# Startup of a fused retention and MLP kernel: values loaded ahead of the half chunk, decay folded into the queries, plain output copies on two engines, and the weights issued behind the values and the queries

## Chip, cores, metric

One core of one Trainium2 chip. The time of a run is the device time of the launch in microseconds (us), and lower is better. All inputs and the output are fp32; the kernel computes in bf16 with fp32 sums. Every run told of here gave a correct result.

## The reference, cut

```python
# q, k, v: (8 batches, 8 heads, 576 tokens, 64); w_ch1: 512 x 2048; w_ch2: 2048 x 512
gamma = 1 - 2.0 ** (-5 - arange(H))                       # one decay per head
ret   = (q @ k.T / 8) * where(rel >= 0, gamma ** rel, 0)  # rel = position of query - position of key
x     = concat_heads(ret @ v)                             # (8, 576, 512)
u     = x + mix_tokens(x, U, V)                           # token mixing of rank 32
out   = u + relu(u @ w_ch1) @ w_ch2
```

`gamma ** rel` splits into `gamma ** t` for the query and `gamma ** -t` for the key. The kernel multiplies the keys by `gamma ** -t`. The factor `gamma ** t` may go on the queries before the scores, or on the output after them.

Of the kernel before, what the change touches and what calls it, by code (L numbers as in the profile page):

```python
# [34 lines left out]
def kernel(  # L35
# [79 lines left out]
    def early_consts():  # L115
        make_identity(nc, ident)
        nc.gpsimd.memset(lnb, math.log(scale))
        nc.gpsimd.iota(
            posU, pattern=[[2 * P, 4], [1, 2], [0, H]], base=0, channel_multiplier=2,
            allow_small_or_imprecise_dtypes=True,  # L120
        )
        nc.gpsimd.iota(
            iotaU, pattern=[[-1, 2], [1, P]], base=0, channel_multiplier=-2,
            allow_small_or_imprecise_dtypes=True,
        )
        nc.gpsimd.iota(
            pos, pattern=[[P, NI], [0, H]], base=0, channel_multiplier=1,
            allow_small_or_imprecise_dtypes=True,
        )
        make_upper_triangular(nc, tri, val=1.0, diag=True)  # L130
        for h in range(H):
            nc.vector.memset(lngt[:, :, h], lng[h])
        nc.vector.tensor_scalar_add(posU[:, 2:4], posU[:, 2:4], -float(4 * P - HALF))
        nc.vector.tensor_tensor(
            out=posU.rearrange("p u j h -> p (u j) h"),
            in0=lngt[:, 0:8, :], in1=posU.rearrange("p u j h -> p (u j) h"), op=ALU.mult)
        nc.scalar.activation(out=vscaleU, in_=posU, func=AF.Exp, bias=lnb, scale=-1.0)
        nc.vector.tensor_scalar(
            out=triU[0:HALF], in0=iotaU[0:HALF], scalar1=0.0, scalar2=None, op0=ALU.is_ge)
        nc.vector.tensor_scalar(  # L140
            out=triU[HALF:P], in0=iotaU[HALF:P], scalar1=-float(P), scalar2=None,
            op0=ALU.is_ge)
        nc.vector.tensor_scalar_add(pos[:, J + 1:NI, :], pos[:, J + 1:NI, :], -float(S))
        nc.vector.tensor_scalar_add(pos[HALF:P, J, :], pos[HALF:P, J, :], -float(S))
        nc.vector.tensor_tensor(out=lngt, in0=lngt, in1=pos, op=ALU.mult)
        nc.scalar.activation(out=qscale, in_=lngt, func=AF.Exp, bias=0.0, scale=1.0)
        nc.scalar.activation(out=vscale, in_=lngt, func=AF.Exp, bias=lnb, scale=-1.0)
        nc.vector.tensor_copy(out=triH[0:HALF], in_=tri[0:HALF, 0:HALF])
        nc.vector.tensor_copy(out=triH[HALF:P], in_=tri[HALF:P, HALF:P])
        nc.vector.memset(U_E[:, J, :], 0.0)  # L150
        nc.vector.memset(U_O[0:HALF, 0, :], 0.0)
        nc.vector.tensor_copy(out=fan, in_=ident[0:R, None, 0:R].to_broadcast([R, 4, R]))
        nc.vector.tensor_copy(out=swap[:, 0:HALF], in_=ident[:, HALF:P])
        nc.vector.tensor_copy(out=swap[:, HALF:P], in_=ident[:, 0:HALF])
        nc.vector.memset(V4[:, 0:HALF], 0.0)
        nc.vector.memset(V4[:, HALF + S:], 0.0)
        nc.vector.memset(sblk, 0.0)
# [97 lines left out]



    def prep_v(pr, i, rows=slice(0, P)):
        c = ch[pr, i]
        if "v" not in c:  # L260
            c["v"] = v_pool.tile([P, H, D], BF16, tag="v", name="vt")
        scale_rows(c["v"][rows], c["f", 2], i, rows, nc.gpsimd)



# [380 lines left out]
        else:  # L646
            eng.tensor_copy(out=o, in_=f)  # L647

    def scale_u(u, hh, eng):
        o, f = unit_views(u, 1, hh)  # L650
        eng.tensor_tensor(
            out=o, in0=f,
            in1=vscaleU[:, u, :, 4 * hh:4 * hh + 4].rearrange("p j h -> p h j")[
                :, :, :, None].to_broadcast([P, 4, 2, D]),
            op=ALU.mult,
        )
# [101 lines left out]
                start=False, stop=True, skip_group_check=True,  # L758
            )

    def XS_u(u, c0=0, c1=2):
        i0, n = unit_i0(u) + c0, c1 - c0
        nc.vector.tensor_tensor(
            out=st["x", 0][:, i0:i0 + n, :].rearrange("p s (h d) -> p s h d", d=D),
            in0=un[u]["po"][:, c0:c1, :].rearrange("p s (h d) -> p s h d", d=D),
            in1=qscale[:, i0:i0 + n, :, None].to_broadcast([P, n, H, D]), op=ALU.mult,
        )

    def ST_u(u, rows, acc, start):
        for hp in range(NHP):  # L770
            for jj in range(2):
                nc.tensor.matmul(
                    acc[:, hp, :], un[u][1][rows, jj, hp * P:(hp + 1) * P],
# [2 lines left out]
                    skip_group_check=True,  # L776
                )

    def Sblk(acc, slot):
        for hl in range(2):  # L780
            r = slice(hl * HALF, (hl + 1) * HALF)
            nc.scalar.activation(
                out=sblk[r, slot, :, hl * D:(hl + 1) * D],
                in_=acc[r, :, hl * D:(hl + 1) * D], func=AF.Copy)

    def T_J(r):
        c = ch[0, J]
# [77 lines left out]
        return ps_s.tile([P, NHP, P], FP32, tag="pss", name="pss")  # L865

    def cast_unit(u):
        for hh in range(2):
            scale_u(u, hh, nc.gpsimd)
        for hh in range(2):  # L870
            cast_u(u, 0, hh, nc.gpsimd)

    def startup():
        load_u(0, (1, 0))
        load_v_rows()
        load_u(1, (1, 0))
        load(0, J, (1, 0), seg=0)
        load_u(0, (2,))
        load_u(1, (2,))
        load(0, J, (2,), seg=0)  # L880
        load_u_rows()
# [16 lines left out]
        SC_u(0, 0, ps_sc, "psc")  # L898
        mask_u(0, 0)
        cast_unit(1)  # L900
        load_w1(0, 2)
        for u in (0, 1):
            for hh in range(2):
                cast_u(u, 2, hh, nc.gpsimd)
        load_w1(2, 4)
        prep_v(0, J, LO)
        load_w1(4, 6)
        cast_urows()
        load_w1(6, 8)
        cast_qk(0, J, HI, nc.gpsimd, nc.gpsimd)  # L910
        prep_v(0, J, HI)
        T_u(1, 1, nc.scalar)
        SC_u(0, 1, ps_o, "po")
        mask_u(0, 1)
        SC_off(0, ps_sc, "psc")
        warm(3)
        T_u(1, 0, None)
        cast_qk(0, J, LO, nc.scalar, nc.vector, decay=True)
        SC_off(1, ps_o, "po")
        warm(4)  # L920
        SC_u(1, 0, ps_sc, "psc")
        mask_u(1, 0)
        SC_u(1, 1, ps_o, "po")
        mask_u(1, 1)
        T_J(LO)

        acc1 = pss_tile()
        acc2 = ps_big.tile([P, NHP, P], FP32, tag="big", name="pss2")
        ST_u(0, ALL, acc1, True)
        Sblk(acc1, 1)  # L930
        RV_u(0, 0)
        RV_u(0, 1)
        ST_u(0, ALL, acc2, True)
        RV_off()
        XS_u(0)
        SC_J(LO)
        mask_J(LO)
        ST_u(1, LO, acc1, False)
        Sblk(acc1, 2)
        ST_u(1, ALL, acc2, False)  # L940
        Sblk(acc2, 3)
        for u in (2, 3):
            for hh in range(2):
                scale_u(u, hh, nc.gpsimd)
            load_w1(4 * u, 4 * u + 4)
            for hh in range(2):
                cast_u(u, 0, hh, nc.gpsimd)
            if u == 3:
                load_w2(0)
                load_w2(2)  # L950
            cast_u(u, 2, 0, nc.gpsimd)
            cast_u(u, 2, 1, nc.gpsimd)
        for f in range(4, NF, 2):
            load_w2(f)
        RV_u(1, 0)
        RV_u(1, 1)
        QS_u(1, 0, 1)
        QS_u(1, 1, 2)
        XS_u(1)
        RV_J(LO)  # L960
        QS_J(3)
        XS_J(LO)

# [30 lines left out]
    def first_stretch():  # L994
# [13 lines left out]
        make_u()  # L1008
        SC_J(HI)
        mask_J(HI)  # L1010
        y(1)
        acc = pss_tile()
        ST_J(HI, acc)
        Sblk(acc, 0)
# [107 lines left out]
```

## The kernel before: what the change touches

The batches go in pairs. Everything here concerns the first pair. Its tokens are four **units** of 256 (units zero and one of the first batch, two and three of the second), and a **half chunk** of 64 tokens at the end of each batch (`J`; `LO` of the first batch, `HI` of the second). SyncE loads keys, queries and values of a unit as six pieces of 128x512 fp32 (256 KB). GpSimd turns them into bf16 and also issues the loads of the weights. An engine works through its list in order, so **a weight load that stands behind a cast in GpSimd's list is issued only when that cast has had its data**.

`w_ch1` is consumed in 16 slices, f = 0 to 15, of 256 KB each in fp32; `load_w1(a, b)` loads slices a to b-1. I number its calls in the order of their slices: the first piece is (0, 2), the third (4, 6). `y(n)` issues the matmuls of the next n slices for the first batch. They fill TensorE between the attention steps of units two and three. When all 16 are done, the "second expansion" begins (the 128x384 matmuls, for the second batch). The position of its first matmul, 54.57 us before, is my yardstick for all that lies ahead of it.

```python
def startup():
    load_u(0, (1, 0)); load_v_rows(); load_u(1, (1, 0))     # SyncE: 1 keys, 0 queries, 2 values
    load(0, J, (1, 0), seg=0)                               # half chunk, keys and queries
    load_u(0, (2,)); load_u(1, (2,)); load(0, J, (2,), seg=0)
    ...                                                     # then all of units two and three
    cast_unit(0)                     # GpSimd: scale keys, cast queries
    ...
    cast_unit(1)
    load_w1(0, 2)                    # first piece of weights
    for u in (0, 1):
        for hh in range(2):
            cast_u(u, 2, hh, nc.gpsimd)                     # values
    load_w1(2, 4)
    prep_v(0, J, LO)
    load_w1(4, 6)                    # third piece
    cast_urows()
    load_w1(6, 8)
    cast_qk(0, J, HI, nc.gpsimd, nc.gpsimd)
    prep_v(0, J, HI)
    ...
    for u in (2, 3):
        for hh in range(2):
            scale_u(u, hh, nc.gpsimd)                       # keys
        load_w1(4 * u, 4 * u + 4)                           # (8, 12), then (12, 16)
        for hh in range(2):
            cast_u(u, 0, hh, nc.gpsimd)                     # queries
        if u == 3: load_w2(0); load_w2(2)
        cast_u(u, 2, 0, nc.gpsimd); cast_u(u, 2, 1, nc.gpsimd)

def XS_u(u, c0=0, c1=2):             # output of a unit, times gamma ** t, PSUM to bf16
    nc.vector.tensor_tensor(out=x[...], in0=po[...], in1=qscale[...], op=mult)

def first_stretch():
    T_J(HI); y(1); make_u(); SC_J(HI); mask_J(HI)
    y(1)
    ST_J(HI, acc); Sblk(acc, 0)      # state of the half chunk
    def unit(u, ...):
        T_u(u, 1, nc.vector)         # transposes of the keys
        T_u(u, 0, nc.scalar)         # transposes of the queries
        y(2)
        SC_u(u, 0, ...); mask_u(u, 0)
        y(1); ...; SC_u(u, 1, ...); y(1); ...
    unit(2, ...); y(1); unit(3, ...); y(1); ...             # cut
```

## Time and profile before

| | before |
|---|---|
| time, median of 3 runs | 326.94 us (326.61 to 327.01) |
| span of the profiled run | 326.0 us |
| TensorE busy | 315.1 us (97%), full from 72 us on |
| outputs of unit zero begin | 16.66 us |
| first slice of the expansion (f = 0) | 24.12 us |
| wait for unit two's queries | 0.94 + 1.41 us, ending at 30.02 |
| TensorE at half clock | once, 30.0 to 33.4 us |
| second expansion begins | 54.57 us |

Positions are from the start of the profiled span. The profiled run took 327.84 us and is not among the three. Weight loads are issued by GpSimd at 12.05, 18.05, 20.17, 21.37, 26.43 and 36.59 us. The lines that carry the rest stand in the prediction.

### The profile page before, as it was taken

What the parts mean: (1) busy time and instruction counts of PE and PEld (TensorE: products, weight loads), DVE (VectorE), ACT (ScalarE), POOL (GpSimd) and SP (SyncE); (2) the same over time, 40 slices, a digit from 0 to 9 for tenths busy, and PEclk for the clock granted to TensorE, in tenths of its full rate; (3) what the DMA queues carried; (4) which work ended last, traced back from release to release, by engine and by line L of the source; (5) the groups of instructions that cost most, each with busy time, mean ns of one, the idle gap of its engine ahead of it and who ended that gap; (6) DMA issues with size and microseconds to landing.
All of it is one profiled execution on the core that took longest, in us unless ns stands there. A gap on an engine that the chain in (4) does not pass through costs nothing.

```text
span 326.0 us, 9119 instructions
## 1 busy us (share of the span) xinstructions
PE 315.1 (97%) x3886; PEld 171.5 (53%) x3886; DVE 169.7 (52%) x331; ACT 144.0 (44%) x326; POOL 101.8 (31%) x169
## 2 busy tenths in 40 slices
PE   8997999999999999999999999999999999999996
PEld 3573545765444444456744444457644444467544
DVE  7662554636645477546754477556744475510012
ACT  3755556894010385048810484058800572047400
POOL 7786752423112733142321523142221500110000
PEclk9998999999999999999999999999999999999999
DMA  7999999995994999979996599969997440340012
GB/s 217 243 198 255 264 201 203 207 193 90 224 206 113 260 171 185 206 182 173 199 202 161 140 183 205 208 157 176 191 202 166 111 68 1 101 112 0 2 74 87
DMA packets 152376, 53.30 MB, mean 163 GB/s; under 512 B 132016, under 2 KB 149808, under 8 KB 152336
## 3 DMA queue, kind: packets, MB, share of 16 engines
q1 hardware_dynamic: 144512, 40.40, 65.1%
q0 software_dynamic: 7824, 12.32, 16.2%
q8 instruction: 30, 0.49, 0.7%
q14 instruction: 10, 0.08, 0.1%
HBM read 36.85 MB, written 9.44 MB: 142 GB/s over the span
## 4 chain that ended last, share of the span: by engine, by line
PE 71%; DMA 15%; SPq 5%; ACT 3%; POOL 2%; DVE 2%; issue 1%; DVEq 0%; POOLq 0%
PE ps_y L565 36%; PE ps_y L531 27%; DMA stage_t<-in_v_dram 8%; DMA stage_t<-in_k_dram 4%; SPq L629 3%; SPq L227 2%; PE pp L312 2%; DVE u L480 2%; DMA stage_t<-in_q_dram 2%; DMA qkT<-qk 1%; ACT y L536 1%; PE pp L332 1%; POOL vt L288 1%; PE ps_y L576 1%; PE pp L344 1%
## 5 line engine op out<-in xcount | busy, mean ns | idle before, releaser
L531 PE MATMUL ps_y<-uT,w_sb 128*128 128x256 bf16 (+2 forms) x768 | 134.3, 328 | 1.6 <-ACT y L536 1.1
L536 ACT ACTIVATE y<-ps_y 128x384 bf16<-128x384 f32 (+2 forms) x192 | 89.6, 491 | 96.1 <-PE ps_y L531 95.0
L565 PE MATMUL ps_y<-w_sb,y 128*128 128x512 bf16 x560 | 126.5, 380 | 0.0
L531 PEld LDWEIGHTS <-w_sb 128*128 128x128 bf16 x768 | 72.7, 98 | 50.3 <-issue 5.0
L565 PEld LDWEIGHTS <-y 128*128 128x128 bf16 x560 | 52.6, 98 | 61.1
L288 POOL TENSOR_TENSOR vt<-stage_t,vscale 64x256 bf16<-64x256 f32 (+1 forms) x81 | 50.3, 621 | 68.7 <-DMA stage_t<-in_v_dram 49.8
L554 DVE TENSOR_TENSOR o_sb<-ps_y,u 128x512 f32<-128x512 f32 (+2 forms) x38 | 25.2, 664 | 82.4 <-PE ps_y L565 80.1
L557 POOL DMA_DIRECT2D out_dram<-o_sb x31 | 17.2, 555 | 108.4 <-DVE o_sb L554 102.6
L320 DVE TENSOR_TENSOR ret<-pp,triH 128x512 bf16<-128x512 f32 x27 | 18.7, 692 | 28.2 <-PE pp L344 20.4
L480 DVE TENSOR_TENSOR u<-ph,xt 128x768 bf16<-128x768 f32 (+2 forms) x24 | 21.8, 951 | 5.9 <-PE ph L474 5.9
L453 ACT ACTIVATE a_sb<-pa 128x128 bf16<-128x128 f32 x8 | 2.2, 278 | 43.8 <-PE pa L447 43.8
L360 DVE TENSOR_TENSOR xt<-pp,qscale 128x512 bf16<-128x512 f32 x27 | 18.6, 689 | 4.7 <-PE pp L344 4.2
L279 DVE CAST qk<-stage_t 64x256 bf16<-64x256 f32 x54 | 19.7, 366 | 1.2
L399 DVE TENSOR_TENSOR s_sb<-AB,Af 64x256 bf16<-64x256 f32 x42 | 17.7, 422 | 2.1 <-ACT s_sb L394 1.5
L354 DVE COPY q<-qkT 64x256 bf16<-64x256 bf16 x48 | 14.0, 293 | 7.5 <-DMA qkT<-qk 6.5
L280 ACT ACTIVATE qk<-stage_t 128x512 bf16<-128x512 f32 x27 | 16.8, 622 | 0.1
L701 DVE TENSOR_TENSOR ret<-psc,triU 128x1024 bf16<-128x1024 f32 x8 | 9.6, 1219 | 10.6 <-PE psc L693 10.6
L392 ACT ACTIVATE Af<-AB 128x256 f32<-128x256 f32 x24 | 9.2, 385 | 7.9 <-PE AB L374 7.4
L647 POOL CAST qk<-stage_t 128x512 bf16<-128x512 f32 x16 | 9.8, 623 | 5.5 <-DMA stage_t<-in_v_dram 2.9
L277 ACT ACTIVATE qk<-stage_t 128x256 bf16<-128x256 f32 x27 | 11.1, 410 | 0.0
L312 PEld LDWEIGHTS <-qkT 64*64 64x64 bf16 x432 | 5.6, 107 | 9.9 <-issue 8.7
L191 PE MATMUL pw<-ident 128*128 128x512 bf16 x27 | 8.8, 473 | 1.4 <-POOL ident masks.py:199 1.4
(120 smaller groups left out, 212.1 us busy)
## 6 DMA issues: line engine op xcount, KB each, us to landing
stage_t<-in_k_dram SPq DMA_DIRECT2D x32, 256.0 KB, 5.0
stage_t<-in_q_dram SPq DMA_DIRECT2D x32, 256.0 KB, 5.5
stage_t<-in_v_dram SPq DMA_DIRECT2D x32, 256.0 KB, 6.0
out_dram<-o_sb POOLq DMA_DIRECT2D x31, 256.0 KB, 3.4
w_sb<-in_moe_w_ch_dram POOLq DMA_DIRECT2D x12, 256.0 KB, 8.1
stage_t<-in_k_dram SPq DMA_DIRECT2D x8, 128.0 KB, 3.8
stage_t<-in_q_dram SPq DMA_DIRECT2D x8, 128.0 KB, 3.4
stage_t<-in_v_dram SPq DMA_DIRECT2D x8, 128.0 KB, 3.6
```

The lines of the kernel that those rows point to most:

```text
L279: nc.vector.tensor_copy(out=o[to, hl], in_=f[fr, hl])
L280: nc.scalar.activation(out=c["qk"][:, 0, :], in_=c["f", 0].rearrange("p h d -> p (h d)"), func=AF.Copy)
L288: nc.gpsimd.tensor_tensor(out=o[to, hl], in0=f[fr, hl], in1=w[fr, hl, :, None].to_broadcast([n, NHP, D]), op=ALU.mult)
L320: nc.vector.tensor_tensor(out=ret.rearrange("p a b i -> p a (b i)").rearrange("p a (b i) -> p a b i", i=D), in0=pp[:, :, 0:NHP * D].rearra ...
L360: nc.vector.tensor_tensor(out=st["x", pr][:, i, :].rearrange("p (hp hl d) -> p hl hp d", hl=2, d=D), in0=pp[:, :, NHP * D:2 * NHP * D].rea ...
L399: nc.vector.tensor_tensor(out=S_[half(x), 1, :], in0=Bk[half(1 - x)], in1=Af[half(1 - x), now, :], op=ALU.add)
L480: nc.vector.tensor_tensor(out=st["u", par][:, i0 - base:i0 - base + n, w].rearrange("p s (c d) -> p c s d", c=2), in0=ph[k][:, :, 0:n, :], ...
L531: nc.tensor.matmul(ps[:, 0:n, :], w1_sb[:, cc, f * P:(f + 1) * P], st["uT", par][:, c0:c0 + n, cc, :], start=(cc == 0), stop=(cc == NCC - 1),)
L536: nc.scalar.activation(out=st["y1", par][:, f, c0 * P:(c0 + n) * P], in_=ps[:, 0:n, :].rearrange("p s t -> p (s t)"), func=AF.Relu)
L554: nc.vector.tensor_tensor(out=o_sb[:, 0:n], in0=ps[:, 0:n], in1=st["u", par][:, c, w], op=ALU.add)
L557: (nc.sync if last else nc.gpsimd).dma_start(out=out_flat[r0:r0 + P, w], in_=o_sb[:, 0:n])
L565: nc.tensor.matmul(ps, st["y1", par][:, f, c * P:(c + 1) * P], w2_sb[:, f, :], start=(f == 0), stop=(f == NF - 1),)
```

## The change

The intent is to shorten the startup and remove the wait for unit two's queries. Values come earlier, the multiply on the way out of PSUM becomes two copies on two engines, unit one (the second unit) is accumulated by halves of the heads, and the first weights leave the loads of the values and queries alone. The core of the diff:

```diff
+        nc.scalar.activation(out=posU, in_=posU, func=AF.Exp, bias=0.0, scale=1.0)   # gamma ** t
     def cast_unit(u):
-        for hh in range(2):
-            scale_u(u, hh, nc.gpsimd)
-        for hh in range(2):
-            cast_u(u, 0, hh, nc.gpsimd)
+        for j in (1, 0):
+            for hh in range(2):
+                scale_u(u, j, hh, nc.gpsimd)
     def XS_u(u):
+        if u < 2:
+            nc.scalar.activation(out=st["x", 0][:, i0, :], in_=un[u]["po"][:, 0, :], func=AF.Copy)
+            nc.vector.tensor_copy(out=st["x", 0][:, i0 + 1, :], in_=un[u]["po"][:, 1, :])
+            return
     def startup():
         load_u(1, (1, 0))
+        load_u(0, (2,))
         load(0, J, (1, 0), seg=0)
-        load_u(0, (2,))
         load_u(1, (2,))
         ...
         cast_unit(1)
-        load_w1(0, 2)
-        for u in (0, 1):  ...cast values...
-        load_w1(2, 4)
-        prep_v(0, J, LO)
-        load_w1(4, 6)
-        cast_urows()
-        load_w1(6, 8)
-        cast_qk(0, J, HI, nc.gpsimd, nc.gpsimd)
-        prep_v(0, J, HI)
+        ...cast values of unit zero, later of unit one; half chunk's values on VectorE...
+        for hh in range(2):
+            ...state and outputs of unit one, by head halves...
+        load_w1(0, 2)
+        cast_urows()
+        load_w1(2, 4)
+        cast_qk(0, J, HI, nc.gpsimd, nc.gpsimd)
+        prep_v(0, J, HI)
         for u in (2, 3):
             ...scale keys...
-            load_w1(4 * u, 4 * u + 4)
+            if u == 3:
+                load_w1(8, 12)
             ...cast queries...
-            if u == 3:
-                load_w2(0)
-                load_w2(2)
+            if u == 2:
+                load_w1(4, 6)
+                load_w1(6, 8)
+            else:
+                load_w1(12, 16)
     def first_stretch():
         mask_J(HI)
-        y(1)
+        y(2)
         acc = pss_tile()
```

Not only the first weights move: the third and fourth pieces go behind the casts of unit two's queries. The kernel also does one slice more, three in place of two, ahead of unit two's transposes.

## The prediction

> **What bounds the kernel now.** I read the page first, parts 2 and 4, then the table of engine times by stretch, then the first 75 us of the timeline and of the chain of waits. Part 2:
>
> ```profile
> PE   8997999999999999999999999999999999999996
> PEclk9998999999999999999999999999999999999999
> DMA  7999999995994999979996599969997440340012
> ```
>
> A slice is 8.15 us. TensorE is full from about 72 us to the end, so nothing that the change does there can count; its work is the same to the matmul (one warm-up matmul fewer). The only dips of TensorE and of its clock lie in the first five slices, where all of the change lies. The stretches of 6 us:
>
> ```profile
> 18.00:24.00 6.00, 5.73 (x135) 4.59 (x132) 3.60 (x5) 2.91 (x8) 5.58 (x10) 1.00 1.11 208
> 24.00:30.00 6.00, 3.55 (x31) 1.68 (x30) 2.25 (x5) 3.33 (x9) 4.38 (x6) 1.00 1.24 262
> 30.00:36.00 6.00, 5.98 (x58) 2.94 (x58) 1.23 (x1) 3.25 (x5) 2.70 (x4) 0.72 1.19 269
> ```
>
> The columns are TensorE, weight loads, VectorE, ScalarE, GpSimd, granted clock, DMA share and GB/s. From 24 to 30 us TensorE does only 3.55 us of work, and from 30 to 36 us it has a granted clock of 0.72. Over 0 to 72 us its busy times sum to 65.6 us, so 6.4 us is all the idle time that there is. Why it idles:
>
> ```profile
> 28.32 0.29 PE L662 MATMUL pst<-ident,qk 128*128 128x128 bf16 x2 [0.94 <-POOL qk L647]
> 29.34 0.62 POOL L647 CAST qk<-stage_t 128x512 bf16<-128x512 f32 x1 [1.07 <-DMA stage_t<-in_q_dram]
> 30.02 0.82 PE L662 MATMUL pst<-ident,qk 128*128 128x128 bf16 x6 [1.41 <-POOL qk L647]
> 30.63 3.26 PE L531 MATMUL ps_y<-uT,w_sb 128*128 128x512 bf16 x8
> ```
>
> TensorE waits for GpSimd's cast of the queries of unit two (the third of four), which waits for their load, landed at 29.3 us. After it, eight 128x512 matmuls take 3.26 us, where four take 1.04 us elsewhere; the low clock costs about 1.2 us here and 1.7 us in all (0.28 of 6 us). So this hole costs some 2.35 + 1.7 = 4 us, the largest prize. Earlier, in the startup:
>
> ```profile
> 15.35 2.34 DVE L701 TENSOR_TENSOR ret<-psc,triU 128x1024 bf16<-128x1024 f32 x2
> 16.66 0.64 PE L720 MATMUL po<-qk,ret 64*128 64x64 bf16 x32
> 19.18 1.03 POOL L252 TENSOR_TENSOR vt<-stage_t,vscale 64x512 bf16<-64x512 f32 x1 [0.38 <-DMA stage_t<-in_v_dram]
> 20.82 1.22 DVE L763 TENSOR_TENSOR xt<-po,qscale 128x1024 bf16<-128x1024 f32 x1 [0.59 <-PE po L755]
> 24.12 1.10 PE L531 MATMUL ps_y<-uT,w_sb 128*128 128x512 bf16 x4 [0.33 <-ACT uT L990]
> ```
>
> From 16.1 to 23.1 us TensorE goes through its startup list with no gap over 0.1 us. It is bound there by its own work once the first mask of unit one has ended (16.56 us; the output tile of unit zero takes that PSUM place, and its first matmul starts at 16.66). The expansion starts at 24.12 us. There is a second bound, in the chain that ended last:
>
> ```profile
> 37.13 12.82 DMA stage_t<-in_v_dram
> 58.29 5.21 DMA stage_t<-in_v_dram
> 65.77 3.56 DMA stage_t<-in_k_dram
> 71.90 2.77 PE ps_y L531 x20
> ```
>
> Before 71.9 us the chain is loads, not TensorE, though TensorE loses only 0.65 us there. A TensorE that comes earlier would wait for these loads of the second batch pair.
>
> **What the Trainium skill says.** (1) "GPSIMD Engine Reference", section 3.1, gives two-input elementwise work on GpSimd about 2.6 cycles per element, because both inputs share a read port, and the best one-input loop 1.8. The trace agrees in direction: the scaling of 128x512 takes 1.058 us and the cast 0.616 us. (2) "PSUM — Partial Sum Buffer", section on bank collisions, says that ScalarE and VectorE must not read the same bank and quadrant at once, but different banks are free. The two halves of the output tile are 128x512 fp32, a bank each. Still the built program makes the VectorE copy wait for the ScalarE copy, so they do not run side by side; the trace has the same pattern where L674 waits 1.34 us for L673. (3) "TensorE: Matmul & The Clock Gate", Part 1, says that the clock halves after an idle window of about 3.4 us and stays so for a window. The trace has one stretch at 0.5, 3.4 us long, after the hole at 28 to 30 us, which had some transposes in it, so it agrees about the length of the slow stretch. (4) "DMA: Bandwidth & Descriptors", section "Queues, rings and completion order", says that each DMA engine takes turns between its queues by packet. The trace agrees: while weights are queued on GpSimd's queue, 512 KB of fp32 lands every 2.8 to 2.9 us (23.56, 26.49, 29.30 us), about 180 GB/s[...].
>
> **The change, part by part.**
>
> Decay in the queries. Four casts of 0.616 us become scalings of 1.058 us on GpSimd. Unit zero's queries end at 8.37 instead of 7.83 us (+0.54); unit one's at 12.56 instead of 12.11 us. Each step after follows: first transposes and scores +0.55, mask zero 10.9, the transposes of unit one's queries 13.2 (12.60 before, a warm-up lies between), their two serial copies end 15.36 (14.76), scores 15.4 (14.81), first mask of unit one 15.95 to 17.15. So the outputs of unit zero start at 17.25 instead of 16.66 us: **+0.6 us on the path**.
>
> Outputs as plain copies. One VectorE multiply of 1.23 us becomes a ScalarE copy of 0.59 and a VectorE copy of 0.69 us, serial: 1.28 us. No gain, and the half chunk's output copy on ScalarE waits behind it: about +0.35 us at the tail.
>
> Values of the half chunk on VectorE. The GpSimd scaling (1.03 us, done 20.22) becomes one of 0.77 us (the like of L240), behind mask, copies and half-chunk masks, done about 21.3 us. Its matmuls, at 20.72 before, come at 21.35. This is mostly the same shift, plus 0.2 us. Sum: the expansion starts at about 25.2 instead of 24.12 us, **+1.1 us**.
>
> Loads. Until 12 us the loads are the same, but the first weights (512 KB of fp32) move from 12.05 to about 17.2 us, and the third and fourth pieces (1 MB) to behind the queries of unit two, about 26.4 us. Values of unit zero land at 12.4 and 13.4 instead of 14.2 and 15.1, which TensorE hardly needs earlier. What counts is the end of unit two's queries. Between 11.44 and 29.29 us before, 4.9 MB went through (276 GB/s); without 1 MB of weights the same takes 14.2 us, so these queries land at about 25.7 and are cast by 26.4. TensorE asks for them at 29.2. **The hole of 2.35 us and its slow clock go: about -4 us.**
>
> What takes its place. A fifth slice of weights (f = 4) is in the third piece, issued 26.4. All six pieces before took 5.5 to 8.7 us to land, so 31.9. TensorE, having done f = 0 to 3, asks for it at 30.6: **a new wait of 1.3 us**. The piece for f = 8 to 11 is issued at about 31.5, behind the fourth (lands 34.8), and needs 5.8 us at 180 GB/s: 40.6; TensorE asks at 39.5: **another 1.1 us**.
>
> Sum: +1.1 - 4 + 1.3 + 1.1 = about **-0.5 us** at 42 us of the trace. I check this with positions: the scores of unit three came at 42.3 us with eight slices done; now they come at 42.4 with nine, each 0.86 us, so -0.75 us. The rest is full TensorE, but for the loads at 69 us, which could take half of it or give another half. I take -0.9 us, leaning a little on the clock staying whole.
>
> **Rivals.**
> 1. The weights are in time. The pieces for f = 4 and f = 8 land before they are asked for. For: SyncE's loads are then further ahead, and GpSimd's queue gets over half of the bandwidth when it has a backlog. Against: every piece took 5.5 us or more. Then -3 us, unless the loads at 69 us hold it: 323.5 to 325.
> 2. The weights are later. The fourth to sixth pieces are queued 5 us later than before, each behind a GpSimd cast that waits for a load. For: the slice of f = 8 was landed 6 us ahead of its use before, so all of that slack is used. Each wait of over 2 us can bring the half clock back for 3.4 us, 1.7 us more. Then +2 to +4 us: 329 to 331.
> 3. Loads bound all up to 72 us. The bytes are the same, and only the dip of DMA share at 17 to 20 us (0.7 to 0.8 against 1.25) can be won, about 1.1 us; the last weights end about 3 us later, since GpSimd's queue begins later. For: the chain of waits names loads. Against: TensorE lost only 0.65 us to them. Then 326 to 328 whatever the startup does.
>
> **Range and chances.** The middle is 326.0 us. Rival 1 sets the low side, 2 and 3 the high side; both are some 2.5 us off, so 323.4 to 328.8. To be faster by over 2%, 6.5 us, nearly all of the idle and slow-clock time (6.4 + 1.7) would have to go: 2%. Slower by 6.5 us needs two long waits for weights with the clock halved: 2%. Within 2%: 96%.
>
> **What would show it.** Right: GpSimd's third and fourth scalings end at about 8.4 us; outputs of unit zero start at 17.2; the expansion starts at 25 us; unit two's queries land before 27 us and TensorE does not wait for their cast; there are waits of 1 to 2 us before the slices f = 4 and f = 8; the VectorE output copy begins where ScalarE's ends. Wrong: an expansion that starts at 24.1 or sooner (then the serial chain was not what set the startup, and the gain is 1 us larger); no wait before f = 4 and f = 8 (rival 1); waits over 2 us there with clock under 1.0 after them (rival 2); a wait of several us at 70 us with no hole before it (rival 3).

## The result

| | before | after |
|---|---|---|
| time, median of 4 runs, the profiled one among them | 326.98 us (326.61 to 327.84) | 332.08 us (331.12 to 333.15) |
| span of the profiled run | 326.0 us | 329.5 us |
| outputs of unit zero begin | 16.66 us | 17.64 us |
| first slice | 24.12 us | 25.99 us |
| wait for unit two's queries | 2.35 us | none |
| wait before slice f = 4 | none | 3.16 us |
| second expansion begins | 54.57 us | 58.25 us |

The ratio is 1.0153 (95% interval 1.0108 to 1.0198). A ratio is the mean time of one kernel's fast runs over that of the other's of the same rounds, so not quite the ratio of the medians. The kernel became about 1.5% slower: inside the 2% class, but 3.3 us above the top of the range.

The page of the kernel after, TensorE, its clock and the DMA share in slices of 8.2 us:

```profile
PE   7797798999999999999999999999999999999996
PEclk9999799999999999999999999999999999999999
DMA  7999999975992999998998599868996542340012
```

TensorE's dip has not gone. It was in the fourth slice and is now in the fourth and fifth, with the reduced clock in the fifth; the second slice, which is the startup, has fallen from 9 to 7. From the eighth slice on the row is as before. By stretches of 6 us (after the window's bounds and its length: TensorE, weight loads, VectorE, ScalarE, GpSimd, then granted clock, DMA share, GB/s):

```profile
12.00:18.00 6.00, 4.89 (x119) 3.29 (x113) 4.13 (x5) 4.93 (x8) 4.06 (x6) 1.00 1.09 164
24.00:30.00 6.00, 5.46 (x68) 2.75 (x68) 2.06 (x4) 3.86 (x9) 3.88 (x5) 1.00 1.22 280
30.00:36.00 6.00, 2.84 (x23) 1.48 (x22) 0.69 (x1) 2.64 (x5) 6.00 (x9) 0.92 1.27 245
```

24 to 30 us is now well filled (5.46, was 3.55), as intended. 30 to 36 us is empty in its place (2.84, was 5.98). The timeline of the kernel after at that point:

```profile
28.84 0.61 POOL L648 CAST qk<-stage_t 128x512 bf16<-128x512 f32 x1 [0.53 <-DMA stage_t<-in_q_dram]
29.40 0.81 POOL L197 DMA_DIRECT2D w_sb<-in_moe_w_ch_dram  x1
...
30.77 1.03 PE L532 MATMUL ps_y<-uT,w_sb 128*128 128x512 bf16 x4
34.95 1.86 PE L532 MATMUL ps_y<-uT,w_sb 128*128 128x512 bf16 x4 [3.16 <-DMA w_sb<-in_moe_w_ch_dram]
```

Read it from the top. The last queries of unit two land and are cast at 28.84. Only then can GpSimd issue the third piece of weights, at 29.40. TensorE is through f = 3 at about 31.8 and waits until 34.95 for slice f = 4 of that piece. That slice then takes 1.86 us instead of 1.03, at half clock. The chain of work that ended last names the same four steps (start, duration, what):

```profile
19.90 8.89 DMA stage_t<-in_q_dram
28.84 0.56 POOL qk L648
29.40 5.51 DMA w_sb<-in_moe_w_ch_dram
34.95 1.86 PE ps_y L532 x4
```

The startup after:

```profile
17.64 0.64 PE L721 MATMUL po<-qk,ret 64*128 64x64 bf16 x32 [0.18 <-DVE ret L702]
...
18.89 0.60 ACT L766 ACTIVATE xt<-po 128x512 bf16<-128x512 f32 x1 [0.36 <-PE po L747]
19.52 0.69 DVE L768 CAST xt<-po 128x512 bf16<-128x512 f32 x1 [0.81 <-ACT xt L766]
...
25.99 1.10 PE L532 MATMUL ps_y<-uT,w_sb 128*128 128x512 bf16 x4 [0.34 <-ACT uT L1001]
```

VectorE's copy begins where ScalarE's ends (18.89 + 0.60) and says so (`<-ACT xt`): the two halves do not run side by side. There is also a wait that I had not foreseen, ahead of the second expansion, in the kernel after and, second, in the one before:

```profile
58.25 1.46 PE L532 MATMUL ps_y<-uT,w_sb 128*128 128x384 bf16 x8 [1.15 <-ACT uT L506]
```
```profile
54.57 1.46 PE L531 MATMUL ps_y<-uT,w_sb 128*128 128x384 bf16 x8 [0.18 <-ACT uT L505]
```

The profiled loss closes by these terms: first slice +1.87, the query wait -2.35, a wait of 0.20 before f = 2, the wait before f = 4 +3.16, the wait at 58 us 1.15 - 0.18 = +0.97. The sum is +3.85. The yardstick moved by 58.25 - 54.57 = 3.68, and the span by 3.5. Each profiled run has one stretch of half clock ahead of 58 us, so that cancels there. The first term is the difference of two single traces. Three edits of each kernel that change nothing ahead of 19 us give its scatter: first slice at 24.12, 24.63, 24.44 and 24.06 us before (with b_fill, b_w68late, b_w4late), and at 25.99, 25.86, 25.68 and 25.62 after (with a_y1, a_warm, a_w34early). The means differ by 1.5 us, and the starts of unit zero's outputs, 16.84 and 17.41 on average, by 0.57.

Over all runs the clock does not cancel. The mean clock of a run shows how many stretches of 3.4 us at half clock it had: none near 1.0, one near 0.995, two (or one of twice the length) near 0.99. Over 43 further runs of the kernel before, on five chips, the mean time was 327.15 us at 1.0 (12 runs), 328.06 at 0.995 (20) and 329.94 at 0.99 (11). The four runs after had 0.993, 0.989, 0.995 and 0.990: one or two stretches, never none. **The times of the same kernel before thus spread over 325.6 to 330.7 us**, and its medians by chip over 327.8 to 329.2. Ratios below are against runs on the same chip.

### The profile page after: what moved, and what is told of

Same layout as the page of the kernel before. It is cut to its first block, busy times and chain, and to the rows that moved or that the text cites. A ratio compares the mean times of both kernels' runs of the same rounds, so it can differ in the third digit from the quotient of the medians.

```text
span 329.5 us, 9122 instructions
## 1 busy us (share of the span) xinstructions
PE 314.5 (95%) x3885; PEld 170.7 (52%) x3885; DVE 169.0 (51%) x333; ACT 144.4 (44%) x327; POOL 103.4 (31%) x169
## 4 chain that ended last, share of the span: by engine, by line
PE 80%; DMA 8%; ACT 4%; SPq 3%; DVE 2%; issue 1%; POOL 1%; DVEq 0%
PE ps_y L566 36%; PE ps_y L532 35%; DMA stage_t<-in_q_dram 3%; SPq L630 2%; DMA stage_t<-in_v_dram 2%; PE pp L313 2%; DMA w_sb<-in_moe_w_ch_dram 2%; DVE u L481 2%; ACT y L537 1%; DMA qkT<-qk 1%; PE pp L333 1%; PE ps_y L577 1%; PE pp L345 1%; PE AB L375 1%; PE pa L448 1%
## 5 line engine op out<-in xcount | busy, mean ns | idle before, releaser
L280 DVE CAST qk<-stage_t 64x256 bf16<-64x256 f32 x54 | 19.5, 360 | 2.0 <-DMA stage_t<-in_k_dram 0.8
L192 PE MATMUL pw<-ident 128*128 128x512 bf16 x26 | 7.9, 446 | 1.4 <-POOL ident masks.py:199 1.4
L652 POOL TENSOR_TENSOR qk<-stage_t,vscaleU 128x512 bf16<-128x512 f32 x8 | 8.4, 1062 | 2.3 <-DMA stage_t<-in_k_dram 1.4
```

The costliest lines, as they stand in the source:

```text
L280: nc.vector.tensor_copy(out=o[to, hl], in_=f[fr, hl])
```

## The experiments

Sixteen kernels ran. Names with `a_` are edits of the kernel after, `b_` of the kernel before, and `c_` are combinations. The theories:

- **Weights:** the loss is the schedule of the weights, above all pieces three and four behind the queries' casts.
- **Startup:** the later first slice (+1.87 us) is what costs.
- **Slice:** the slice spent early is missing at 57 us.
- **Clock:** the half-clock stretch after the wait, not the wait, is the cost.

### The third and fourth pieces early: a_w34early

```diff
         load_w1(2, 4)
+        load_w1(4, 6)
+        load_w1(6, 8)
         ...
-            if u == 2:
-                load_w1(4, 6)
-                load_w1(6, 8)
-            else:
+            if u == 3:
                 load_w1(12, 16)
```

> The changed kernel with the third and fourth weight pieces (slices 4 to 7) issued right behind the second, ahead of the half chunk's casts, not behind unit two's queries. Theory W (the wait for the third piece took the place of the wait for the queries): the piece lands at about 31 instead of 34.9 us, no wait before slice 4; unit two's queries land 1 to 1.5 us later than 28.8, so some 1 us of the old wait comes back; total 327.5 to 329.5. Rival B (only the bytes ahead of TensorE count, whatever their order): what the slice gains the queries lose, total stays 331 to 333. Rival S (the loss is all startup): unchanged, 331 to 333, with no change before 26 us.

Measured: 333.48 us, ratio 1.0167 (1.0114 to 1.022). The wait before f = 4 was gone (that slice at 31.45 us), and a longer one stood before f = 8:

```profile
44.63 3.59 PE L532 MATMUL ps_y<-uT,w_sb 128*128 128x512 bf16 x8 [5.43 <-DMA w_sb<-in_moe_w_ch_dram]
```

The fifth piece was still behind unit three's key scalings, so it was issued at 36.55 and landed at 44.58. Curing one piece moved the wait to the next. The times expected under the theory of the weights, 327.5 to 329.5, did not come: this edit alone cures nothing. The run had 6.8 us at half clock.

### The first piece back in its place: a_w1first

```diff
         cast_unit(1)
+        load_w1(0, 2)
         cast_u(0, 2, 0, nc.gpsimd)
         ...
-        load_w1(0, 2)
         cast_urows()
```

> The changed kernel with the first weight piece back at its old place, ahead of the value casts (about 13 us instead of 18.2). Theory D (between 13 and 20 us SyncE's small loads cannot fill the DMA engines, so the first piece is free there): it lands at about 19, unit two's queries land 1 to 1.9 us earlier (27 to 27.8), the third piece is issued that much earlier, the wait before slice 4 falls from 3.2 to about 1.7 us; total 329.5 to 330.5. Rival B (bytes alone): the values and the half chunk land about 1 us later, the expansion starts about 1 us later, queries as they are; total 331 to 333.

Measured: 328.43 us, ratio 1.0007 (0.9974 to 1.004); one of the four runs, 332.66 us, counted as slow and is not in the ratio. Unit two's queries landed at 25.0 us, not at 28.79, though 512 KB more were queued ahead of them. The third piece was issued at 27.08, and its slice came at 33.46:

```profile
33.46 1.04 PE L532 MATMUL ps_y<-uT,w_sb 128*128 128x512 bf16 x4 [2.73 <-DMA w_sb<-in_moe_w_ch_dram]
```

A wait of 2.73 us, with no half clock in this run. So a large part of the loss depends on where the first piece lies, though less surely than the ratio says. The run left out is the only one of the study; with it the four average 329.26 us, 0.4% over the kernel before. It lies 4.5 us above the other three, and its clock of 0.995 stands for 1.7 of these at most.

What moved through the DMA engines, by queue (packets, MB, share of the time of 16 engines; shares can add up to over 100%). q1 is SyncE's queue, q0 GpSimd's. A piece of weights counts there as 0.26 MB, the bf16 that is written. From 12 to 18 us, the kernel after and then a_w1first:

```profile
q1 hardware_dynamic: 3118, 0.96, 107.4%
```
```profile
q1 hardware_dynamic: 3124, 0.97, 96.9%
q0 software_dynamic: 519, 0.26, 39.0%
```

From 18 to 24 us, in the same order:

```profile
q1 hardware_dynamic: 2488, 0.92, 66.3%
q0 software_dynamic: 508, 0.25, 34.9%
```
```profile
q1 hardware_dynamic: 3202, 1.30, 97.6%
q0 software_dynamic: 125, 0.06, 8.0%
```

From 12 to 18 us SyncE's loads moved as much without the first piece (0.96 MB) as beside it (0.97). **With the piece away, the other loads did not take over its bandwidth.** From 18 to 24 us they moved 0.92 MB beside weights, and 1.30 nearly without. In the kernel after the first two pieces, issued at 18.24 and 19.54 us, were in flight until 25.17 and 28.52, and the last queries of unit two took 8.89 us from issue to landing. In a_w1first the first piece had landed at 19.36, the second was issued only at 20.83, and these queries took 4.96 us. So the change, by issuing the first piece later, put it **beside the queries**. This compares two traces. In a_w1all, below, where the first piece is early too but three more are in flight beside the queries, they landed at 30.41 us.

### The extra slice back: a_y1

```diff
         mask_J(HI)
-        y(2)
+        y(1)
```

> The changed kernel with one slice, as before, ahead of the half chunk's state, not two. Theory W: slice 4 is then asked for one score group later, so the wait falls by some 0.4 us, and one slice more is left to fill the wait at 56 us (1.2 us, was 0.2 us before the change), so about 1 us there: total 1.2 to 2 us below the changed kernel of the same rounds. Rival: the extra slice fills the hole and its absence costs: same or slower.

Measured: 331.68 us, ratio 1.010 (1.0062 to 1.0138). The wait at the second expansion fell to that of the kernel before:

```profile
60.52 1.46 PE L532 MATMUL ps_y<-uT,w_sb 128*128 128x384 bf16 x8 [0.18 <-ACT uT L506]
```

So the extra slice is the cause of that wait of 1.15 us. But the slice was then missing earlier: TensorE waited 0.81 us for the queries and 4.89 us for f = 4. The slice decides where TensorE waits, and hardly how long.

### The startup's decay undone: a_nodecay

```diff
     def XS_u(u):
-        if u < 2:  ...two plain copies...
     def cast_unit(u):
+        ...scale keys, cast queries, as before...
```

> The changed kernel without the decay in the queries: they are cast as before and the outputs of units zero and one take one VectorE multiply. Theory W: the expansion starts 0.6 to 1 us earlier than 26.0, but slice 4 still waits for the third piece that lands at 34.9, so the wait grows by as much and the total stays within 0.5 us. Rival S (startup chain is the loss): total 0.6 to 1.5 us lower.

Measured: 331.97 us, ratio 1.0118 (1.0076 to 1.0159). TensorE was ready for the first slice at 24.67 us, over 1 us earlier than in the kernel after. It waited 0.97 us for the first piece of weights, and 4.75 us for the third. A faster startup ran into the weights, whose third piece landed at 35.99 us. This speaks against the startup theory.

### The first piece late in the kernel before: b_w1late

```diff
-        load_w1(0, 2)
         for u in (0, 1):
             ...cast values...
-        load_w1(2, 4)
+        load_w1(0, 2)
         prep_v(0, J, LO)
-        load_w1(4, 6)
+        load_w1(2, 4)
         cast_urows()
+        load_w1(4, 6)
         load_w1(6, 8)
```

> The kernel before, with only the first weight piece moved behind the four value casts (issued at about 17 us, not 12), the second and third each one place later, all else as it was. Theory D: the startup does not change (the expansion starts at 24 us, or waits a little for the piece), but the 512 KB now lie in the busy time from 20 to 29 us, so unit two's queries land at 30 to 31 us, not 29.3, and the wait grows: total 1 to 4 us over before. Rival B (bytes alone) or 'the weights were in the way of the values': same total or lower.

Measured: 328.73 us, ratio 0.9996 (0.9956 to 1.0036). Unit two's queries landed at 26.68 us, so the expectation of 30 to 31 failed. In this kernel the late first piece did not delay the queries. TensorE waited 0.60 + 0.26 us for them, and then 1.11 + 0.86 + 0.26 us in unit three. From 8 to 24 us it moved as much as the kernel before, 3.52 MB and 3.55. By queue it was SyncE's loads that made up for the piece, with 3.23 MB in place of 2.88 (weights 0.26 in place of 0.64). In this order of loads, then, they did take over its place, though four pieces were issued between 17.8 and 22.4 us. A late first piece alone does not cost time, then, and the loss seen against a_w1first belongs to the kernel after as a whole.

### Decay in the queries alone: b_decay

```diff
     def cast_unit(u):
-        ...scale keys, cast queries...
+        for j in (1, 0):
+            for hh in range(2):
+                scale_u(u, j, hh, nc.gpsimd)
     def XS_u(u, ...):
+        if u < 2:  ...ScalarE copies one half, VectorE the other...
```

> The kernel before with only the decay in the queries and the outputs of units zero and one as two copies. Startup chain: the expansion starts 0.6 to 1.2 us later than 24.1. Theory W/D: the wait for unit two's queries (landed at about 29.3 whatever GpSimd does before) shrinks by as much, total within 0.7 us of before. Rival S: total 0.6 to 1.5 us over before.

Measured: 328.22 us, ratio 0.9963 (0.9914 to 1.0012). The outputs of unit zero began at 17.4 us and the first slice at 25.25, 1.1 us later than before, which is the size predicted. In the time no loss is seen: the interval ends at 1.0012, and the startup theory asked for 0.6 to 1.5 us, 1.0018 at least. So that theory is refuted here. That TensorE loses this time ahead of a wait that it would have had anyway is the explanation I expected, but the profiled run, the slowest of its four, does not show it: the wait there did not shrink but grew, to 0.99 + 2.04 us, since the queries were cast only at 31.23.

### The fourth and sixth pieces later in the kernel before: b_w68late

```diff
         cast_urows()
-        load_w1(6, 8)
         ...
-            load_w1(4 * u, 4 * u + 4)
+            if u == 2:
+                load_w1(6, 8)
+            else:
+                load_w1(12, 16)
             ...cast queries...
+            if u == 2:
+                load_w1(8, 12)
```

> The kernel before with the fourth weight piece (slices 6 and 7) issued behind unit two's key scaling, where the fifth was, and the fifth behind the query casts. Its 512 KB then no longer stand before unit two's queries: by the bytes (270 GB/s) these land 1.9 us sooner, at about 27.4, the wait of 2.35 us falls to about 0.7 and with it perhaps the slow clock (1.7 us). Slices 6 and 7 are asked for at about 36 us and land at 33 to 35, slice 8 at about 39 against 40. Total 1.5 to 3.5 us under before; if slice 8 waits, the same or 1 us over.

Measured: 326.71 us (324.84 to 329.42), ratio 0.9943 (0.9872 to 1.0014). The queries landed at 28.14 us instead of 29.29, which is 1.15 us for 512 KB moved behind them. TensorE waited 0.24 + 0.64 us, and the second expansion began at 51.79, 2.8 us earlier. The best single time of the study is here, but the four runs had 0, 1, 0 and 2 half-clock stretches, and the interval holds 1.

### All weights at the places of the kernel before: a_w1all

```diff
         cast_unit(1)
+        load_w1(0, 2)
         ...
-        load_w1(0, 2)
-        cast_urows()
         load_w1(2, 4)
+        load_w1(4, 6)
+        cast_urows()
+        load_w1(6, 8)
         ...
+            load_w1(4 * u, 4 * u + 4)       # and load_w2 as before
```

> The changed kernel with all weight pieces where the kernel before has them. Theory W/D: no wait for weights; the expansion starts at about 25.5; unit two's queries land at about 29 and TensorE asks for them at about 29.5, so a wait of 1 us or less; 1 us more is lost at 56 us for the slice that was used up. Total within 1.5 us of before (the changed kernel is 5 us over it). Rival S: stays 1.5 to 3 us over before.

Measured: 327.9 us, ratio 0.9982 (0.9936 to 1.0027). All the rest of the change was kept: values ahead, decay, copies on two engines, head halves, the extra slice. The first slice began at 25.64 us, as late as in the kernel after, and the wait was again the one for the queries:

```profile
31.13 0.51 PE L663 MATMUL pst<-ident,qk 128*128 128x128 bf16 x6 [1.25 <-POOL qk L648]
```

The second expansion began at 54.19 us (54.57 before). **This decides between the theories:** the loss is in the schedule of the weights, and all other parts together are worth nothing either way, to within about 0.6%.

### Is it the clock? a_warm

```diff
-            y(2)
+            y(1)
+            if u == 2:
+                ...12 matmuls of 128x512 on the identity, result unused...
+            y(1)
```

> The changed kernel with twelve warm-up matmuls of 128x512 (2.6 us at full clock) between slices 3 and 4, where TensorE waited 3.2 us for the third weight piece. Their result is never read. If the slow clock after the wait is part of the loss, it goes: slices 4 to 6 run at full clock and the total is 1.7 to 3.4 us below the changed kernel (ratio to before 1.005 to 1.010, not 1.015). If the wait alone is the loss, the ratio stays at about 1.015. If the piece comes earlier than in that trace, the warm-ups themselves cost up to 2.6 us.

Measured: 331.93 us, ratio 1.014 (1.0091 to 1.0189). The matmuls lie between f = 3 and f = 4, where TensorE waits. Three of the four runs had a clock of 0.999 to 1.0, and took 332.60, 331.25 and 330.88 us. The fourth, the slowest, had one stretch, and is the one that was profiled. After the twelve matmuls TensorE still waited there for the third piece:

```profile
37.01 1.04 PE L532 MATMUL ps_y<-uT,w_sb 128*128 128x512 bf16 x4 [2.37 <-DMA w_sb<-in_moe_w_ch_dram]
```

These three runs average 331.6 us, 4.4 us above the 327.15 of the kernel before at full clock. So the wait itself costs, and the clock theory explains at most the difference between runs of one kernel.

### Filling the wait of the kernel before with the slice: b_fill

```diff
         mask_J(HI)
-        y(1)
+        y(2)
         ...
-            y(2)
+            y(1 if u == 2 else 2)
```

> The kernel before with the second slice of unit three's... of the third unit's pair (slice 2) moved ahead of the half chunk's state, that is into the wait for the queries; no slice is used up. The wait of 2.35 us falls by one slice, to about 1.4; total 0.9 us under before, and 2.6 under it if the clock then stays whole.

Measured: 326.81 us, ratio 0.9972 (0.9928 to 1.0016). The wait for the queries fell to 1.51 us, with 0.53 us before the scores. It had no half-clock stretch in three of four runs. A gain of 0.3% is suggested, not shown.

### Two combinations that did not settle: c_fill68 and b_vfirst

c_fill68 is b_fill and b_w68late together. b_vfirst is the kernel before with one part of the change alone:

```diff
         load_u(1, (1, 0))
-        load(0, J, (1, 0), seg=0)
         load_u(0, (2,))
+        load(0, J, (1, 0), seg=0)
```

> The same, and the fourth weight piece behind unit two's key scaling and the fifth behind its query casts: the version meant to beat both. The queries land near 28 us, the wait is under 0.5 us, no slow clock, no wait at 56 us; slices 6 and 8 in time. Total 2.5 to 4 us under before (ratio 0.988 to 0.992). If slice 8 then waits for the fifth piece: ratio 0.995 or more.

> The kernel before with only the load order changed: the values of unit zero ahead of the half chunk's keys and queries. TensorE's startup is set by the first mask of unit one and by its own work after it, so nothing is to be had: total within 0.5 us of before. Were the values what held the startup, 0.5 to 1 us less.

Measured: c_fill68 326.23 us (325.31 to 329.73), ratio 0.9977 (0.9931 to 1.0023); its profiled run, the slowest of six, waited 2.98 us for values of unit three. b_vfirst 327.17 us, ratio 0.9982 (0.994 to 1.0024). Neither is told apart from the kernel before.

### The change with its weights one place earlier: a_w34fix

Here the first two pieces stay late, as in the change, but the third to sixth are each issued one place earlier:

```diff
         load_w1(2, 4)
+        load_w1(4, 6)
         cast_qk(0, J, HI, nc.gpsimd, nc.gpsimd)
         ...
             ...scale keys...
-            if u == 3:
-                load_w1(8, 12)
-            ...cast queries...
             if u == 2:
-                load_w1(4, 6)
                 load_w1(6, 8)
             else:
                 load_w1(12, 16)
+            ...cast queries...
+            if u == 2:
+                load_w1(8, 12)
```

> The changed kernel, first two weight pieces late as in the change, but the third right behind the second, the fourth behind unit two's key scaling, the fifth behind its query casts, the sixth behind unit three's key scaling: one place earlier each than in the change. If the loss is that pieces three to six stand behind casts that wait for loads, the third lands at about 31 us and the fifth at about 38 to 40, no wait over 1 us before slices 4 and 8, ratio to before 0.996 to 1.004. If the late first piece is the loss by itself, ratio 1.010 or more.

Measured: 327.4 us (326.64 to 328.89), ratio 0.9961 (0.9907 to 1.0015), all four runs at clock 1.0. The third piece was issued by 19.5 us and landed at 29.3, the fourth at 34.13, the fifth at 38.37. TensorE's waits:

```profile
34.17 1.04 PE L532 MATMUL ps_y<-uT,w_sb 128*128 128x512 bf16 x4 [0.34 <-DMA w_sb<-in_moe_w_ch_dram]
...
38.80 0.28 PE L663 MATMUL pst<-ident,qk 128*128 128x128 bf16 x2 [0.49 <-POOL qk L648]
39.92 0.51 PE L663 MATMUL pst<-ident,qk 128*128 128x128 bf16 x6 [0.84 <-POOL qk L648]
```

0.34 us for a weight, 1.33 us for unit three's queries, none for unit two's. **With a_w1all this is the proof from the side of the kernel after: the order of four weight loads gives back the whole loss.** It also corrects a reading that a_w1first invites: the first piece need not be early. The kernel before drew slow runs on this chip (see b_w4late), but against the mean of all its 43 runs, 328.29 us, these four (mean 327.59) are not slower either, and c_a34 below repeats the result on another chip.

### The change's late weights in the kernel before: b_w4late

```diff
-        load_w1(4, 6)
         cast_urows()
-        load_w1(6, 8)
         ...
-            load_w1(4 * u, 4 * u + 4)
+            if u == 3:
+                load_w1(8, 12)
             ...cast queries...
+            if u == 2:
+                load_w1(4, 6)
+                load_w1(6, 8)
+            else:
+                load_w1(12, 16)              # load_w2 also as in the change
```

> The kernel before, first two weight pieces as they were, but pieces three to six and the last matrix where the change has them, each behind casts that wait for loads. Unit two's queries land 1.5 to 3 us earlier (26.5 to 28); the third piece is issued at about 28 and lands at 33.5 to 35, slice 4 is asked for at about 30.5: a wait of 3 to 4 us in place of the 2.35 us. Ratio to before 1.003 to 1.010. If it is 1.000 or less, the places of pieces three to six cost nothing without the rest of the change.

Measured: 329.53 us, ratio 1.0006 (0.9943 to 1.007). The queries landed at 27.0 us, 2.3 us earlier for 1 MB moved behind them. TensorE waited only 0.27 us for them, and then:

```profile
35.16 1.89 PE L531 MATMUL ps_y<-uT,w_sb 128*128 128x512 bf16 x4 [4.65 <-DMA w_sb<-in_moe_w_ch_dram]
```

The mechanism is the same in a kernel that has nothing else of the change: one wait taken away, a longer one in its place, and half clock after it. The second expansion began at 57.05 us. The **time** does not confirm a loss. On this chip three of the seven runs of the kernel before had two half-clock stretches (median 328.98), so the comparison is against a slow draw and the interval is wide. From the side of the kernel before, the theory rests on the trace alone.

### Towards a better version: c_a34 and c_b68v

c_a34 is a_w34fix with one slice of unit two's filler kept back (`y(1 if u == 2 else 2)`). c_b68v is b_w68late with b_vfirst's order of loads.

> a_w34fix (changed kernel, pieces three to six one place earlier) with one slice fewer in unit three's first filler, so that a slice is left for the wait at 56 us, which was 1.15 us in every kernel that used it up and 0.2 us in the others. If that accounting is right, TensorE's wait there falls to 0.2 us and the total is up to 1 us under a_w34fix (ratio to before 0.992 to 0.996); if the slice only moves the wait to the scores of the third unit, ratio as a_w34fix, 0.996.

> b_w68late (kernel before, fourth and fifth weight pieces one place later) with the values of unit zero ahead of the half chunk's keys and queries. If the fewer bytes ahead of unit two's queries are a real gain (b_w68late gave 0.994, unclear), ratio 0.992 to 0.996 with an interval under 1; if it was a lucky draw of the slow-clock windows, 0.997 to 1.001.

Measured: c_a34 327.26 us (6 runs), ratio 0.997 (0.9928 to 1.0012). Its wait at the second expansion was gone, but it waited 1.35 us for unit three's queries and 0.54 us before scores: again the slice only chose the place. c_b68v 326.59 us (325.51 to 327.99, 6 runs), ratio 0.9952 (0.9905 to 0.9999), with a single wait for unit two's queries left:

```profile
29.49 0.51 PE L662 MATMUL pst<-ident,qk 128*128 128x128 bf16 x6 [0.77 <-POOL qk L647]
```

Its second expansion began at 52.41 us. It is some 0.5% faster than the kernel before, with an interval that just excludes 1 (one of sixteen intervals, so a hint), and some 2% faster than the kernel after if the two ratios are divided (0.9952 / 1.0153 = 0.980, over different chips).

## Why the prediction was wrong

**The reading of what bounds the kernel was right.** All of the difference arose ahead of 58 us (3.68 of it, of 3.5 in the span), and nothing came back or was added behind it.

**The query wait went, as predicted.** It was 2.35 us and became none.

**The step that failed is "these queries land at about 25.7".** They landed at 28.79, only half a microsecond earlier than the 29.29 of before (at 28.44, 29.05 and 29.32 in a_nodecay, a_warm and a_y1, which have the same schedule of weights). The step took 1 MB out of all the bytes ahead of them and divided by one rate, 276 GB/s, as though it did not matter when the bytes go. (The rate comes from the fp32 sizes; the profile, which counts weights as bf16, has 227 GB/s from 11.44 to 29.29.) But in the kernel before the first piece had landed at 18.36, ahead of the queries' issue at 20.76 and 21.32, and the change put it beside them. The last queries were issued 1.4 us earlier (19.90) and took 0.9 us longer (8.89, was 7.97). With the first piece back in its place they took 4.96 us and landed at 25.00 (a_w1first), close to where the step had put them. In the edits of the kernel before, one trace each, issuing 512 KB behind the queries brought them forward by about 1.1 us (b_w68late 1.15 us; b_w4late 2.3 us for two), not by the 1.9 us of that division.

**The third piece's wait was named, and mis-sized for that reason.** "Issued 26.4", "lands 31.9" became 29.40 and 34.91, so the wait "of 1.3 us" became 3.16. The load took 5.5 us in this trace, as I had taken it, so the error came in whole from the issue, which hangs on the queries' cast. But 5.5 was the least of the six pieces before, and this was luck: in the three edits that kept this schedule the load took 7.54, 6.95 and 7.30 us, and TensorE waited longer still, 4.89 us (a_y1), 4.75 us (a_nodecay), and 2.37 us left after twelve filling matmuls (a_warm). Their ratios, 1.010 to 1.014 on two chips, also show that the loss comes with the schedule.

**The clock.** "The hole of 2.35 us and its slow clock go: about -4 us" took 1.7 us for the clock as a sure gain. Its stretch only moved, to 35.0 to 38.4 us. Nor was it all in the median to be gained: the profiled run before was the slowest of its four (327.84 us), and the other three, 326.61 to 327.01, are as fast as the runs without a stretch (327.15); their own clock is not on record. I had written the condition myself in rival 2: a wait of over 2 us can bring the half clock back. Rival 2 is what happened: its 329 to 331 us is close to the 332.08 measured, and I gave it too little weight. It named the fourth to sixth pieces, though; the wait came at the third.

**The second new wait, 1.1 us before f = 8, did not come.** TensorE was late enough for that piece. It came, at 5.4 us, in a_w34early, where f = 4 was in time.

**The startup was right in mechanism.** The two serial copies, the later mask and the +0.6 us at the outputs of unit zero (measured +0.98, or 0.57 between the means of four traces) all showed. The +1.1 us at the first slice was +1.87 in the kernel after, +1.5 between the means, +1.2 to +1.5 in two other kernels with the same startup (a_w34fix 25.31, a_w1all 25.64), and +1.1 in b_decay. But counting it in the sum was wrong where a wait for a load follows: a_nodecay took over 1 us of it away and gained nothing that shows. One aside was misread: the copies L673 and L674, called "the same pattern", read two halves of one tile of 128x1024 bf16, 2 KB, which is one bank and not two.

**A term was missing:** the extra slice leaves none for the wait ahead of the second expansion, +0.97 us there (a_y1 shows it). I checked positions at 42 us and not at 57. As a_y1 and c_a34 show, giving the slice back moves the wait rather than removing it.

**Rivals 1 and 3** are refuted: the weights were not in time, and the loads at 70 us cost the same 0.65 us as before.

With the sizes measured, the sum in the prediction's own form is +1.87 - 2.35 + 0.20 + 3.16 + 0.97 = +3.85 us in the profiled run. The medians differ by 5.1 us. The rest is not settled run by run. The profiled run before was the slowest of its four and the profiled run after one of its two faster ones, 331.24 - 327.84 = 3.4 us apart; half-clock stretches, likely fewer in the other runs before and more in two of the others after, can make up the difference. Open is also why the queries of b_w1late landed at 26.68 with a late first piece and three more issued right behind it. SyncE's loads moved 1.27 MB there from 12 to 18 us, against 0.96 in the kernel after; but no run separates this from the order of the small loads and from the later casts that free their buffers.

## What to carry to other kernels

Where an engine both casts what it waits for and issues other loads, moving a load behind a cast ties it to that cast's data: work out its issue from the **latest** landing that the traces allow, not from a mean rate, and compare with the time of first use. Ask also which transfers will be in flight **beside** the load that is waited for: bytes that leave its neighbourhood help, but a piece moved from ahead of it to beside it can take back nearly all that another gives. And a gain ahead of a wait for a load is worth nothing until the load itself comes earlier: look for the next wait in the list before counting it.

## What the Trainium skill lacked or had wrong

- "DMA: Bandwidth & Descriptors", section "Queues, rings and completion order", says how each DMA engine takes turns between queues. It does not say what one queue gains when the other falls silent. Here, from 18 to 24 us, SyncE's queue moved 0.92 MB beside 0.25 MB of weights (after) and 1.30 MB beside 0.06 (a_w1first); but from 12 to 18 us it moved 0.96 MB with no weights at all and 0.97 beside 0.26 MB of them.
- "TensorE: Matmul & The Clock Gate", Part 1, says that the clock's window runs freely and that the transition depends on its phase, which agrees. Its rule, "no PE-idle gaps >~3.4µs", was not enough here: waits of 0.94 + 1.41 us (before) and of 3.16 us (after) were followed by a stretch at half clock, and one of 2.73 us (a_w1first) was not. One unchanged kernel had no, one or two such stretches by run, with mean times of 327.15, 328.06 and 329.94 us over 43 runs.
- No page that I found says that the built program may make two engines' copies out of one PSUM tile wait for each other when they read different banks of it. Here the second copy (0.69 us) began only when the first (0.60 us) had ended, in both units, while the two copies to `uT`, out of different PSUM tiles, ran side by side (25.34 and 25.38 us). That the shared tile is the reason is my inference.
